# Attention and a maxout layer on one core: weights scaled by sixes, the first query blocks of four batches ahead, two sets of tokens in turn

## The chip, the core and the metric

The kernel runs on one core of a Trainium2 chip, in one launch. Its engines work side by side and are tied by semaphores: TensorE (PE, with its weight loads PEld), VectorE (DVE), ScalarE (ACT), GpSimd (POOL) and SyncE (SP). DMAs are issued here from SyncE's and from ScalarE's list. The metric is the device time of a run in microseconds.

## The reference

For 8 batches, 8 heads, 576 positions and 64 columns a head, in float32:

```python
scores = scale * np.matmul(q, k.transpose(0, 1, 3, 2))
cum = np.cumsum(np.maximum(s, 0.0), axis=-1)
bias = -(cum[:, :, :, None] - cum[:, :, None, :])
scores = np.where(causal, -1e9, scores + np.minimum(bias, 0.0))
attn = softmax(scores)                                  # over the keys
x = np.matmul(attn, v)  # heads side by side: 4608 tokens of 512 columns
h = np.maximum(np.maximum(x @ w1, x @ w2), x @ w3)      # 512 to 768
return h @ w_out                                        # 768 to 512
```

The four weight matrices arrive as 64-bit numbers, q, k, v and s as float32.

## The kernel before, in words

**Attention.** Two heads make a pair (`g`, four pairs a batch), and a *visit* is one batch, one pair and a list of query blocks of 128 (the fifth block is the last 64 positions). Batches that are in the array `qkv0` (its first dimension is `NB`, 2 before) are visited twice: first for the query blocks 0 and 1 alone (phase 0, 256 tokens), later for the blocks 2, 3 and 4 (phase 1, 320 tokens). The other batches are visited once for all five blocks. A *step* is one query block of one visit; there are 160.

A step runs over the engines in this order: the scores, in high and low parts (`scores`, TensorE, tiles `s`); their maximum (`highest`, VectorE, `nm`); the exponentials (`expo`, ScalarE); the reciprocal of their sum (`ri`, VectorE); the probabilities as a high half (`prh`, ScalarE) and a low half (`prl`, VectorE), both float16; their transposes by DMA from SyncE's list into `ph` and `pl` (tags `pTh`, `pTl`, one buffer for each phase); and, once a phase of a visit is complete, the products with v (`values`, TensorE, tile `av`), which ScalarE and VectorE bring into the token tile `x`, again as a high and a low half. Two score buffers are there, so the scores of step t+2 are written when those of step t are free.

**Experts.** When the four pairs of a batch's phase are done, its 256 or 320 tokens are a *set* (`add_set`), named by batch and phase: 2_1 is batch 2, phase 1. A set has 18 groups of 12 matmuls (`pm`, L593: six blocks `ft` of 128 hidden columns, three matrices each), of which ScalarE fetches the first (`m`, L607), VectorE maximises in the other two (L610), ScalarE and GpSimd split the result (`hh` L599, `hl` L600); and 4 output groups of 18 matmuls (`po`, L635), brought out by ScalarE (L643) and written by DMA. The groups wait in a list, `queue`, in the order of their sets. `run_group` takes the first, provided that its weights are there. How many go into a step is rationed: each step adds `STEP_NS` = 4800 ns less its own estimated time on TensorE to an account, and groups are issued while it is above zero. What is left after the last step runs at the end.

**Weights.** 24 blocks of 128 x 512 numbers in 64 bits, 18 for the hidden layer and 6 for the output. Each is loaded (`load_w`, tile `r`), put together as float32 from its two words (`decode1` on ScalarE L489, `decode2` on VectorE, three instructions, L494, L495, L498), and split into two float16 halves (`decode3` on ScalarE L552; `decode4`, on VectorE L566 or, for each third block, on GpSimd L563, L564). Ahead of the split stands a power of two by which they are scaled: from products of the blocks with themselves (`gram1`, TensorE, tile `gr`, L508), their maximum (`gram2`), and its spread over all partitions by a small matmul (`power`, tile `gm`). There is one scale for the 18 blocks and one for the 6, so no block of the 18 is split before all of them are loaded and decoded.

**Order.** Nothing is scheduled by a tool: each engine's list is written out by the loop over the steps and by two tables, `early` and `todo`, which name what else is done in a step (loads, preparations, weights). `begun`, `split` and `fetched` are the steps at which the weights' decode, split and load stand. SyncE's list holds the transposes, most loads of q, k and v and the writes of the outputs; the weights are loaded from ScalarE's list, but for the first few.

## Time and profile before

| | |
|---|---|
| median of 3 runs | 979.97 us (979.19 to 982.53) |
| the profiled run's own time | 981.28 us |
| its span, first to last instruction | 979.5 us |
| mean granted clock of TensorE in it | 0.948 |
| TensorE matmul, weight load busy | 867.9 us (89%), 657.7 us (67%) |
| VectorE, ScalarE, GpSimd busy | 566.5 us, 571.7 us, 182.3 us |
| DMA | 107.41 MB in all, 12.3 MB of them by ScalarE's queue |

The page gives each engine's busy time, and the same over 40 equal slices of the span in tenths. Matmuls are pipelined and overlap, so a time per matmul is better read from a stretch of them end to end than from the mean duration of one. A line such as L610 is a line of the kernel before; the number in brackets behind a busy time counts instructions.

### The profile page before, as it was taken

The page shows a single profiled execution, that of the slowest core. Times are in us where ns is not written, and L with a number is a line of the kernel's source. Part 1 is how long each engine was busy: PE and PEld are TensorE (multiplying, and loading weights), DVE is VectorE, ACT ScalarE, POOL GpSimd, SP SyncE. Part 2 cuts the span into 40 slices and gives each one's busy share as a digit, 9 for nine tenths or more (in the row PEclk, how much of TensorE's full clock was granted, in tenths as well). Part 3 has the DMA queues.
Part 4 walks back from the last instruction along what each step waited for, and adds up shares of the span by engine and source line. Part 5 has one row for each costly group of instructions (what it writes and reads, how often), then busy time and mean ns, then how long its engine had stood idle before and what let it go on. Part 6 is the DMA issues. An engine that isn't in the chain of part 4 may idle for free. (4 is left out here: it accounts for less than half of the span.)

```text
span 979.5 us, 20205 instructions
## 1 busy us (share of the span) xinstructions
PE 867.9 (89%) x7576; PEld 657.7 (67%) x7576; DVE 566.5 (58%) x1184; ACT 571.7 (58%) x1550; POOL 182.3 (19%) x231
## 2 busy tenths in 40 slices
PE   2446779897999959999999999999999999999998
PEld 1334557775666748767777767766776777777876
DVE  6797876656646565656565655555565655454111
ACT  4547666656566565666666666666566666665121
POOL 2003641212103010212121212112121212110111
PEclk9756879999999968999999999999999999999999
DMA  8962345476465565554745463645555474434000
GB/s 298 225 180 52 91 82 127 94 143 126 93 136 117 125 113 92 124 103 99 136 98 122 77 135 80 128 97 118 99 109 122 96 135 85 110 63 96 8 23 27
DMA packets 237810, 107.41 MB, mean 110 GB/s; under 512 B 216656, under 2 KB 225360, under 8 KB 237712
## 3 DMA queue, kind: packets, MB, share of 16 engines
q1 hardware_dynamic: 233680, 93.79, 46.1%
q10 hardware_dynamic: 4032, 12.32, 4.4%
q8 instruction: 60, 0.98, 0.5%
q14 instruction: 38, 0.31, 0.1%
...
## 5 line engine op out<-in xcount | busy, mean ns | idle before, releaser
L593 PE MATMUL pm<-x,w 128*128 128x256 f16 (+1 forms) x3456 | 458.8, 290 | 10.7 <-DVE x L468 5.8
L593 PEld LDWEIGHTS <-w 128*128 128x128 f16 x3456 | 333.8, 99 | 98.0 <-issue 10.6
L404 DVE SCALAR_TENSOR_TENSOR prl<-s,ri,prh 128x512 f16<-128x512 f32 (+3 forms) x288 | 152.8, 568 | 84.4 <-ACT prh L401 54.3
L401 ACT ACTIVATE prh<-s,ri 128x512 f16<-128x512 f32 (+3 forms) x288 | 141.9, 538 | 76.4 <-DVE ri L385 61.2
L600 POOL TENSOR_TENSOR hl<-m,hh 128x256 f16<-128x256 f32 (+1 forms) x96 | 71.4, 744 | 567.2 <-ACT hh L599 561.1
L352 DVE TENSOR_REDUCE nm<-s 128x1 f32<-128x576 f32 (+4 forms) x160 | 128.4, 803 | 63.1 <-PE s L325 57.9
L362 ACT ACTIVATE s<-s,nm 128x512 f32<-128x512 f32 (+4 forms) x288 | 150.6, 523 | 10.2 <-DVE nm L352 6.1
L610 DVE SCALAR_TENSOR_TENSOR m<-pm,m 128x256 f32<-128x256 f32 (+1 forms) x192 | 87.0, 453 | 117.4 <-PE pm L593 101.6
L635 PE MATMUL po<-hh,w 128*128 128x256 f16 (+1 forms) x768 | 151.4, 288 | 0.0
L635 PEld LDWEIGHTS <-w 128*128 128x128 f16 x1152 | 111.3, 99 | 27.4
L635 PE MATMUL po<-hl,w 128*128 128x320 f16 (+1 forms) x384 | 110.6, 288 | 0.0
L599 ACT ACTIVATE hh<-m 128x256 f16<-128x256 f32 (+1 forms) x96 | 42.3, 440 | 105.5 <-DVE m L610 105.3
L321 PE MATMUL s<-qkh 64*128 64x128 f32 (+3 forms) x256 | 56.3, 429 | 49.6 <-DVE prl L404 42.9
L263 POOL TENSOR_TENSOR qkl<-raw,qkh 128x576 fp32r<-128x576 f32 (+1 forms) x36 | 55.0, 1527 | 174.0 <-PE s L325 117.9
L321 PEld LDWEIGHTS s<-qkh 64*128 64x128 f32 x256 | 26.9, 196 | 80.4 <-ACT s L362 42.4
L607 ACT ACTIVATE m<-pm 128x256 f32<-128x256 f32 (+1 forms) x96 | 38.9, 405 | 64.8 <-PE pm L593 62.6
L468 DVE SCALAR_TENSOR_TENSOR x<-av,x 128x256 f16<-128x256 f32 (+1 forms) x64 | 29.0, 453 | 74.4 <-ACT x L467 74.3
L467 ACT ACTIVATE x<-av 128x256 f16<-128x256 f32 (+1 forms) x64 | 26.3, 410 | 75.4 <-PE av L457 75.3
L643 ACT ACTIVATE o<-po,os 128x256 f32<-128x256 f32 (+1 forms) x64 | 31.9, 498 | 51.5 <-PE po L635 48.1
L457 PE MATMUL av<-pl,vh 128*64 128x320 f16 (+3 forms) x384 | 57.1, 283 | 5.3 <-DMA pl<-prl 5.3
L457 PEld LDWEIGHTS <-vh 128*64 128x64 f16 x832 | 45.2, 113 | 23.7 <-issue 17.1
L457 PE MATMUL av<-ph,vh 128*64 128x320 f16 (+3 forms) x384 | 58.2, 291 | 0.1
(120 smaller groups left out, 1028.5 us busy)
## 6 DMA issues: line engine op xcount, KB each, us to landing
...
r<-in_w_dram ACTq DMA_DIRECT2D x20, 512.0 KB, 5.6
...
ph<-prh SPq DMA_TRANSPOSE x192, 3.2
pl<-prl SPq DMA_TRANSPOSE x192, 2.8
```

The source lines that it names most:

```text
L263: nc.gpsimd.tensor_tensor(out=r["lo"][:, cq:c1], in0=r["k"], in1=r["hi"][:, cq:c1].bitcast(F32), op=ALU.subtract)
L321: nc.tensor.matmul(ps[:, j, :nk], lhsT=lhsT, rhs=rt[rows], start=(n == 0), stop=False, skip_group_check=True)
L352: nc.vector.tensor_reduce(out=nm, in_=sc, axis=AX.X, op=ALU.max, negate=True)
L362: nc.scalar.activation(out=sc, in_=sc, func=AF.Exp, bias=nm[:, j:j + 1], accum_out=sm[:, j:j + 1])
L401: nc.scalar.activation(out=hi, in_=src, func=AF.Copy, scale=sc)
L404: nc.vector.scalar_tensor_tensor(out=lo, in0=src, scalar=sc, in1=hi, op0=ALU.mult, op1=ALU.subtract)
L457: nc.tensor.matmul(av[j * D:(j + 1) * D, c0:nq], lhsT=lt, rhs=rt, start=(n < 2), stop=(n >= len(todo) - 2), skip_group_check=True,)
L593: nc.tensor.matmul(pm[:, :nq], lhsT=w[:, wt, kt, :], rhs=xt, start=(n == 0), stop=(n == 3 * NKT - 1))
L599: nc.scalar.activation(out=st["hh"][:, ft, :nq], in_=m1[:, :nq], func=AF.Copy)
L600: nc.gpsimd.tensor_tensor(out=st["hl"][:, ft, :nq], in0=m1[:, :nq], in1=st["hh"][:, ft, :nq], op=ALU.subtract)
L610: nc.vector.scalar_tensor_tensor(out=m1[:, :nq], in0=pm[:, :nq], scalar=HSC, in1=m1[:, :nq], op0=ALU.mult, op1=ALU.max)
L635: nc.tensor.matmul(pm[:, :nq], lhsT=W[18 + ft][:, wt, dt, :], rhs=st[ht][:, ft, :nq], start=(n == 0), stop=(n == 3 * NFT - 1),)
```

## The change

The array `qkv0` holds four batches instead of two (`nb = 4`). Thereby 16 visits of the blocks 0 and 1 stand first, then 16 of the blocks 2, 3 and 4, then the other four batches as before.

The 24 weight blocks are scaled in four chunks of six in the order in which they are used, each chunk with its own power of two. So the first six can be split once they are loaded and decoded, and a hidden block's scale depends on its chunk; a factor (`rel`) on the output weights of that hidden block makes up for it, computed by GpSimd from the four scales. The decode, one block a step or less at first, is spread over the steps -2 to 26, the splits over 10 to 32; the low half is taken by VectorE for all blocks. The raw blocks share 12 buffers instead of having one each, and those from 2 on are loaded from SyncE's list, the last twelve as buffers come free.

`queue` is a list of sets, and `next_group` takes the next group of the first or, where that one's weights are not there, of the second set. The two sets have their own buffers `hh`, `hlo` and `m1`; outputs use the decode's buffers `t`. The token tiles use `x0` to `x5` and the raw buffers. In the visits for the blocks 0 and 1 alone, `ph` and `pl` alternate between two buffers from visit to visit. The spread of a scale (`spread_max`) is a step later than its maximum. In the first 32 steps the account gets 5600 ns a step, and the results of groups are fetched behind a step's `todo` instead of both ahead of it and behind it.

```diff
     def load_start(v, dma):
-        t = wpool.tile([P, 2 * N], F32, tag=f"w{18 + v}", name=f"st{v}")
-        dma(out=t[:, 0:768], in_=qkv0[0, visits[v][1]])
+        g = visits[v][1]
+        t = wpool.tile([P, N], F32, tag=f"r{RAW - NP + v}", name=f"st{v}")
+        dma(out=t, in_=qkv0[0, g, :, 0:512])
+        rv = io.tile([P, QKV - V0], F32, tag=f"rv{g}", name=f"rv{v}")[:, 0:256]
+        dma(out=rv, in_=qkv0[0, g, :, 512:768])
...
     def load_w(i, dma=None):
-        w = wpool.tile([P, 2 * N], F32, tag=f"w{i}", name=f"r{i}")
+        w = wpool.tile([P, 2 * N], F32, tag=f"r{i % RAW}", name=f"r{i}")
...
         if qb in (0, 2):
+            tag = v % 2 if visits[v][2][-1] == 1 else ph
             PT[v, ph] = [
-                att.tile([P, 4 + 4 * ph, PH[ph][1]], F16, tag=f"pT{c}{ph}", name=f"p{c}{t}", bufs=1) for c in "hl"
+                att.tile([P, 4 + 4 * ph, PH[ph][1]], F16, tag=f"pT{c}{tag}", name=f"p{c}{t}", bufs=1) for c in "hl"
             ]
...
-        if k < 2 * NB:
-            return moe.tile([P, 2, 2, nq], F16, tag=f"x{k}", name=name)
-        tag = f"w{10 + (k - 2 * NB) % 8}"
+        tag = f"x{k}" if k < 6 else f"r{(k - 6) % RAW}"
...
-    def gram1(kind, n, ids):
-        gr = ps_m.tile([P, 512], F32, tag="m", name=f"gr{kind}{n}")
-        for a, i in enumerate(ids):
+    def gram1(c):
+        gr = ps_m.tile([P, 512], F32, tag="m", name=f"gr{c}")
+        for i in range(6 * c, 6 * c + 6):
...
+    def scale_w(i):
+        return WS[chunk(i)] if i < 18 else WS["rel", (i - 18) // 2]
...
-        if by_pool(i):
-            ts = moe.tile([P, N], F32, tag="t", name=f"ts{i}", bufs=4)
-            nc.gpsimd.tensor_scalar(out=ts, in0=t, scalar1=sw, scalar2=None, op0=ALU.mult)
-            nc.gpsimd.tensor_tensor(out=w[:, 1], in0=ts, in1=w[:, 0], op=ALU.subtract)
-        else:
-            nc.vector.scalar_tensor_tensor(
-                out=w[:, 1], in0=t, scalar=sw, in1=w[:, 0], op0=ALU.mult, op1=ALU.subtract
-            )
+        nc.vector.scalar_tensor_tensor(
+            out=w[:, 1], in0=t, scalar=scale_w(i), in1=w[:, 0], op0=ALU.mult, op1=ALU.subtract
+        )
...
+        slot = 0 if ph else 1 if b >= NB else b % 2
+        wide = 256 if slot else 320
+        groups = []
...
-                queue.append((lambda ft=ft, i=i: h_group(ft, i), (3 * ft + i,), 12 * nq * NSEC))
+                groups.append((lambda ft=ft, i=i: h_group(ft, i), (3 * ft + i,), 12 * nq * NSEC))
...
+        queue.append(groups)
...
+    def next_group():
+        for groups in queue[:2]:
+            if all(i in W for i in groups[0][1]):
+                return groups
+        return None
+
     def ready():
-        return bool(queue) and all(i in W for i in queue[0][1])
+        return next_group() is not None
 
     def run_group():
-        f, _, c = queue.pop(0)
+        groups = next_group()
+        f, _, c = groups.pop(0)
         f()
         cost[0] -= c
+        if not groups:
+            queue.remove(groups)
...
-    begun = {i: (i - 1) // 2 - 1 for i in range(1, 18)}
-    begun.update({0: -2, 17: 6, 22: 7, 23: 8, 18: 9, 19: 10, 20: 11, 21: 12})
-    split = {i: 8 + i // 3 for i in range(18)}
-    split.update({i: 15 + (i - 18) // 3 for i in range(18, 24)})
+    begun = {0: -2, 1: -1, 2: 1, 3: 3, 4: 4, 5: 5}
+    begun.update({6: 7, 7: 9, 8: 11, 9: 12, 10: 13, 11: 14})
+    begun.update({12: 15, 13: 16, 14: 17, 15: 18, 16: 19, 17: 20})
+    begun.update({18: 22, 19: 22, 20: 23, 21: 23, 22: 24, 23: 25})
+    scaled = {0: 8, 1: 16, 2: 22, 3: 27}
+    split = {i: scaled[i // 6] + 2 + ((i % 6) if i < 6 else (i % 6) // 2) for i in range(NW)}
+    for c, t in scaled.items():
+        soon(t, gram1, c)
+        at(t, gram2, c)
+        soon(t + 1, spread_max, (c, "top"))
+        at(t + 1, wscale, c)
...
-    for i, t in fetched.items():
-        at(t, load_w, i, nc.scalar.dma_start)
+    for i in range(8, RAW):
+        at(max(2 * (i - 8) - 3, 0), load_w, i)
+    for i, t in split.items():
+        if i + RAW < NW:
+            at(t + 1, load_w, i + RAW)
...
-        cost[0] = min(cost[0] + STEP_NS - pe_cost(t), 4000.0)
+        cost[0] = min(cost[0] + (5600.0 if t < 2 * NP * NB else STEP_NS) - pe_cost(t), 4000.0)
...
-        drain()
-        flush()
+        if t >= 2 * NP * NB:
+            drain()
+            flush()
         for f, a in todo.get(t, ()):
             f(*a)
+        drain()
+        flush()
...
-    nb = 2
+    nb = 4
```

How the lists move, at three places. The first is VectorE's list from the maximum of step 5 on (`t` and `r` are a weight block being decoded, `am` a maximum over v, `vl` the low half of v). Before:

```order
L352 TENSOR_REDUCE nm5_465<-s5_464 128x2
L404 SCALAR_TENSOR_TENSOR prl4_508<-s4_377,ri4_505,prh4_507 128x128 x2
L494 TENSOR_SCALAR t9_499<-t9_499 128x512
L495 SCALAR_TENSOR_TENSOR t9_499<-r9_295,t9_499 128x512
L498 SCALAR_TENSOR_TENSOR r9_295<-r9_295,t9_499 128x512
L494 TENSOR_SCALAR t10_501<-t10_501 128x512
L495 SCALAR_TENSOR_TENSOR t10_501<-r10_297,t10_501 128x512
L498 SCALAR_TENSOR_TENSOR r10_297<-r10_297,t10_501 128x512
L290 SCALAR_TENSOR_TENSOR vl2_494<-st2_137,inv0_0_231,vh2_493 128x2x128
```

and of the change:

```order
L360 TENSOR_REDUCE nm5_418<-s5_417 128x2
L413 SCALAR_TENSOR_TENSOR prl4_449<-s4_362,ri4_446,prh4_448 128x128 x2
L500 TENSOR_SCALAR t3_440<-t3_440 128x512
L501 SCALAR_TENSOR_TENSOR t3_440<-r3_153,t3_440 128x512
L504 SCALAR_TENSOR_TENSOR r3_153<-r3_153,t3_440 128x512
L236 TENSOR_REDUCE am4_477<-rv4_254 128x1
L236 TENSOR_REDUCE am4_477<-rv5_383 128x1
L298 SCALAR_TENSOR_TENSOR vl2_435<-rv2_143,inv0_0_243,vh2_434 128x2x128
```

One weight block is decoded in the step where two were, and the blocks 9 and 10 come many steps later. The second place is VectorE's list around step 55 (`m` rows fetch an expert group, `x` a token tile). Before:

```order
L352 TENSOR_REDUCE nm54_4425<-s54_4424 128x1
L404 SCALAR_TENSOR_TENSOR prl53_4462<-s53_4387,ri53_4459,prh53_4461 128x4x128 x2
L468 SCALAR_TENSOR_TENSOR x18_0_4470<-av18_0_4446,x18_0_4470 128x256
L385 RECIPROCAL ri54_4491<-se54_4487 128x1
L352 TENSOR_REDUCE nm55_4474<-s55_4473 128x2
L404 SCALAR_TENSOR_TENSOR prl54_4494<-s54_4424,ri54_4491,prh54_4493 128x512
L404 SCALAR_TENSOR_TENSOR tl54_4495<-s54_4424,ri54_4491,tl54_4495 128x64
```

and of the change:

```order
L360 TENSOR_REDUCE nm54_4327<-s54_4326 128x2
L413 SCALAR_TENSOR_TENSOR prl53_4359<-s53_4250,ri53_4356,prh53_4358 128x3x128 x2
L625 SCALAR_TENSOR_TENSOR m13_0_4_4309<-pm3_0_4_2_4367,m13_0_4_4309 128x256
L298 SCALAR_TENSOR_TENSOR vl23_4346<-rv23_3385,inv1_1_3773,vh23_4345 128x640
L274 SCALAR_TENSOR_TENSOR qkl24_4402<-raw24_4092,qkh24_4350 128x384
L394 RECIPROCAL ri54_4462<-se54_4394 128x2
L360 TENSOR_REDUCE nm55_4381<-s55_4380 128x1
L413 SCALAR_TENSOR_TENSOR prl54_4465<-s54_4326,ri54_4462,prh54_4464 128x4x128 x2
L625 SCALAR_TENSOR_TENSOR m13_0_5_4473<-pm3_0_5_1_4420,m13_0_5_4473 128x256
```

Before, no expert group is in the list between the steps 53 and 58; in the change groups of set 3_0 are. In TensorE's list the change has, of expert groups, the 18 of 0_0 and the 18 of 1_0 before step 31, none in 31 to 33, and then some in every step: the eight output groups of those two sets, 2_0, 3_0, 0_1 and 1_1 but for two output groups by step 80. Before, the sets 0_0, 1_0, 0_1, 1_1, 2_0 and 2_1 stand by step 80. The third place is who issues the weights' loads. Before, ScalarE's list in step 5:

```order
L256 ACTIVATE qkh4_563<-raw4_422 128x256
L489 ACTIVATE t11_566<-r11_299 128x512
L489 ACTIVATE t12_568<-r12_345 128x512
L125 DMA r22_570<-in_w_dram 128x512
L125 DMA r23_572<-in_w_dram 128x512
L401 ACTIVATE prh5_589<-s5_464,ri5_587 128x2x128 x2
```

and of the change SyncE's, in the steps 20 to 22:

```order
L416 DMA_TRANSPOSE ph20_1544<-prh20_1548 128x2x128
L416 DMA_TRANSPOSE pl20_1545<-prl20_1549 128x2x128
L114 DMA rv14_1596<-in_qkv0_dram 128x256
L99 DMA raw13_1598<-in_qkv0_dram 128x512
L129 DMA r20_1608<-in_w_dram 128x512
L129 DMA r21_1610<-in_w_dram 128x512
L416 DMA_TRANSPOSE ph20_1544<-prh21_1668 128x4x128
L416 DMA_TRANSPOSE pl20_1545<-prl21_1669 128x4x128
```

The weights' loads stand between the transposes of one step and the next.

More of the change, by code (lines that the diff above doesn't have):

```diff
@@ L500, in decode2, with chunk, gram2, wscale @@
         )
[L502 to L504 removed]
+    def chunk(i):
+        return i // 6
+    def gram1(c):
+        gr = ps_m.tile([P, 512], F32, tag="m", name=f"gr{c}")
+        for i in range(6 * c, 6 * c + 6):
             top = raw_w[i].bitcast(BF16).rearrange("p (n t) -> p n t", t=4)[:, :, 1]
[L506 to L507 removed]
+            for k in range(NKT):
+                part = top[:, k * P:(k + 1) * P]
                 nc.tensor.matmul(
[L509 to L527 removed]
+                    gr[:, :P], lhsT=part, rhs=part,
+                    start=(i % 6 == 0 and k == 0), stop=(i % 6 == 5 and k == NKT - 1),
+                )
+        WS[c, "gram"] = gr
+    def gram2(c):
+        am = small.tile([P, 1], F32, tag="am1", name=f"amw{c}")
+        nc.vector.tensor_reduce(out=am, in_=WS.pop((c, "gram"))[:, :P], axis=AX.X, op=ALU.max)
+        WS[c, "top"] = power(am, f"w{c}")
+    def wscale(c):
+        mx = small.tile([P, 1], F32, tag="mx", name=f"mxw{c}")
+        nc.vector.tensor_reduce(out=mx, in_=WS.pop((c, "top"))[:, :P], axis=AX.X, op=ALU.max)
+        rt = const.tile([P, 1], F32, name=f"rt{c}")
         nc.vector.tensor_scalar(
@@ L531, in wscale2 @@
         )
-        sw = const.tile([P, 1], F32, name=f"sw{kind}")
+        sw = const.tile([P, 1], F32, name=f"sw{c}")
         nc.vector.reciprocal(out=sw, in_=rt)
         nc.vector.tensor_scalar(out=sw, in0=sw, scalar1=2.0 ** -56, scalar2=None, op0=ALU.mult)
-        WS[kind] = sw
+        WS[c] = sw
         nc.gpsimd.tensor_scalar(out=rt, in0=rt, scalar1=2.0 ** 56, scalar2=None, op0=ALU.mult)
-        WS[kind, "inv"] = rt
-        if kind == "d":
+        WS[c, "inv"] = rt
+        if c == 2:
+            low = const.tile([P, 1], F32, name="low")
+            nc.gpsimd.tensor_scalar(out=low, in0=WS[0], scalar1=WS[1], scalar2=None, op0=ALU.min)
+            nc.gpsimd.tensor_scalar(out=low, in0=low, scalar1=WS[2], scalar2=None, op0=ALU.min)
+            top = const.tile([P, 1], F32, name="top")
+            nc.gpsimd.tensor_scalar(out=top, in0=WS[0, "inv"], scalar1=WS[1, "inv"], scalar2=None, op0=ALU.max)
+            nc.gpsimd.tensor_scalar(out=top, in0=top, scalar1=WS[2, "inv"], scalar2=None, op0=ALU.max)
+            WS["top"] = top
+            for k in range(3):
+                f = const.tile([P, 1], F32, name=f"rel{k}")
+                nc.gpsimd.tensor_scalar(out=f, in0=WS[k, "inv"], scalar1=low, scalar2=None, op0=ALU.mult)
+                WS["rel", k] = f
+        if c == 3:
+            for k in range(3):
+                f = WS["rel", k]
+                nc.gpsimd.tensor_scalar(out=f, in0=f, scalar1=sw, scalar2=None, op0=ALU.mult)
             kw = const.tile([P, 1], F32, name="kw")
             nc.gpsimd.tensor_scalar(
-                out=kw, in0=rt, scalar1=WS["u", "inv"], scalar2=1.0 / HSC, op0=ALU.mult, op1=ALU.mult
+                out=kw, in0=rt, scalar1=WS["top"], scalar2=1.0 / HSC, op0=ALU.mult, op1=ALU.mult
             )
             WS["kw"] = kw
+    def scale_w(i):
+        return WS[chunk(i)] if i < 18 else WS["rel", (i - 18) // 2]
     def decode3(i):
@@ L582, in add_set @@
         u = f"{b}_{ph}"
-        xs = [(t[:, i, 0], t[:, i, 1]) for t in X.pop((b, ph)) for i in range(2)]
+        xs = [(t[:, i, 0, 0:nq], t[:, i, 1, 0:nq]) for t in X.pop((b, ph)) for i in range(2)]
         st = {}
+        slot = 0 if ph else 1 if b >= NB else b % 2
+        wide = 256 if slot else 320
+        groups = []
         def h_group(ft, i):
@@ L726 @@
         w = v - NP
[L727 to L731 removed]
+        at(first[w] + (4 if w % NP == 0 else 2), vmax, v)
     for v in range(NP, len(visits), NP):
@@ L738 @@
                 t = first[v] + 1 + (f is prep5) if v else -1
-            if f is prep5 and v >= NP and v + NP < len(visits):
+            if f is prep5 and v + NP < len(visits):
                 at(t, f, v)
@@ L742 @@
                 continue
-            if f is load and NP <= v < 2 * NP:
+            if f is load and v < NP * NB + 2:
                 t = first[v] - 6
             at(t, f, v, *([nc.scalar.dma_start] if f is load and v < NP + 2 else []))
-    at(8, wscale2, "u")
     for i, t in split.items():
```

80 lines of the change are left out of this document (23 added, 57 removed).

## The prediction

> **What bounds the kernel now.** I read the page's slices first, then busy times by stage.
>
> ```profile
> PE 867.9 (89%) x7576; PEld 657.7 (67%) x7576; DVE 566.5 (58%) x1184; ACT 571.7 (58%) x1550; POOL 182.3 (19%) x231
> PE   2446779897999959999999999999999999999998
> PEclk9756879999999968999999999999999999999999
> ```
>
> TensorE is at nine tenths or more from about 370 us to the end. It is poorly filled in the first seven slices of 24.5 us and again in slice 15 (343 to 367 us). I number a step by its maximum reduction nm (L352) and cut the span at such reductions:
>
> ```profile
> 13.20:127.20 114.00, 8.53 (x16) 0.75 0.56 144
> 127.20:479.80 352.60, 55.47 (x64) 0.94 0.56 115
> 479.80:899.10 419.30, 63.63 (x80) 1.00 0.52 104
> ```
>
> So steps 0 to 15 take 114.0 us (7.1 each), 16 to 79 take 352.6 (5.5), 80 to 159 take 419.3 (5.2), and 80.4 us follow. The engines in smaller stages (columns PE, PEld, DVE, ACT, POOL busy, clock, DMA share, GB/s):
>
> ```profile
> 13.20:34.90 21.70, 10.62 (x69) 8.52 (x70) 19.44 (x45) 14.99 (x43) 1.87 (x2) 1.00 0.99 256
> 34.90:72.80 37.90, 15.83 (x135) 12.81 (x135) 31.12 (x71) 18.22 (x54) 1.68 (x2) 0.59 0.74 195
> 72.80:127.20 54.40, 38.83 (x312) 29.92 (x311) 44.88 (x97) 35.44 (x94) 25.90 (x21) 0.76 0.27 64
> ...
> 164.70:265.40 100.70, 88.92 (x763) 66.50 (x761) 62.01 (x120) 63.20 (x158) 20.49 (x24) 0.97 0.61 124
> 343.10:369.80 26.70, 15.99 (x100) 12.18 (x102) 16.35 (x31) 17.64 (x48) 3.96 (x4) 0.60 0.63 118
> 503.60:609.50 105.90, 102.51 (x935) 77.84 (x933) 61.41 (x131) 66.00 (x184) 18.44 (x23) 1.00 0.53 109
> ```
>
> Three regimes. In the steady state (last row, one batch) TensorE is busy 102.5 of 105.9 us and sets the pace. In the first 114 us VectorE is busy 19.44 + 31.12 + 44.88 = 95.4 us, 84%, and TensorE 57% at clocks down to 0.59. From 343 to 370 us nobody is full. The counts of the expert matmuls (L593) say why:
>
> ```profile
> 13.20:127.20 114.00, 25.87 (x176) 19.25 (x177) 0.75 0.56 144
> 164.70:265.40 100.70, 53.45 (x386) 37.73 (x384) 0.97 0.61 124
> 343.10:369.80 26.70, 0.00 (x0) 0.00 (x0) 0.60 0.63 118
> ```
>
> From 343.1 to 369.8 us not one runs: the list is empty, because batch 2's sets are complete only at its last visit. So TensorE has too little it may do in two places, and its total work does not change with this edit. What the change can win is idle TensorE time.
>
> **Prices on TensorE.** The chain that ended last is nothing but expert work at full clock:
>
> ```profile
> 911.79 17.14 PE pm L593 x156
> 928.93 7.99 PE po L635 x72
> 936.91 29.34 PE pm L593 x216
> 966.25 9.79 PE po L635 x72
> ```
>
> A matmul takes 0.110 us at 256 columns (17.14 / 156, 7.99 / 72) and 0.136 at 320. A group of 12 costs 1.32 or 1.63 us, an output group of 18 2.0 or 2.45, a whole set 31.8 (18 x 1.32 + 4 x 2.0) or 39.1 (29.34 + 9.79). The batch of the steady row holds one of each, 70.9; the other 35.0 us are four visits, 8.75 each, stalls included. For the second half of a visit (query blocks 2 to 4) I use 164.7 to 265.4 us: 17 steps, 5.67 such halves, and besides the 386 matmuls (32 groups, 16 of each width, 47.2 us) four output groups (8.0). That leaves 45.5 us, 8.0 a half, or 5.9 if TensorE's idle 11.8 us are taken off. I take 6.0 for a filled TensorE, so 2.75 for the first half.
>
> **Stage one, steps 0 to 31.** The change visits blocks 0 and 1 of four batches, not two: 32 such steps, with the same 24 weights' decode spread over them. VectorE paid for the old stage, so I price the new one there:
>
> ```profile
> L385 DVE RECIPROCAL ri<-se 128x2 f32<-128x2 f32 x128 | 20.4, 160 | 37.9 <-ACT se L366 37.7
> L352 DVE TENSOR_REDUCE nm<-s 128x2 f32<-128x256 f32 x32 | 13.2, 412 | 10.4 <-PE s L325 10.4
> L352 DVE TENSOR_REDUCE nm<-s 128x2 f32<-128x512 f32 x32 | 21.8, 682 | 6.0 <-PE s L325 5.6
> L404 DVE SCALAR_TENSOR_TENSOR prl<-s,ri,prh 128x128 f16<-128x128 f32 x64 | 19.4, 345 | 12.8 <-ACT prh L401 9.3 <-DMA pl<-prl 2.8
> L404 DVE SCALAR_TENSOR_TENSOR prl<-s,ri,prh 128x256 f16<-128x256 f32 x64 | 27.8, 476 | 11.0 <-ACT prh L401 6.2 <-DMA pl<-prl 4.8
> L266 DVE SCALAR_TENSOR_TENSOR qkl<-raw,qkh 128x256 fp32r<-128x256 f32 x4 | 2.2, 548 | 0.0
> L290 DVE SCALAR_TENSOR_TENSOR vl<-rv,inv,vh 128x256 f16<-128x256 f32 x4 | 1.8, 474 | 0.0
> L228 DVE TENSOR_REDUCE am<-rv 128x1 f32<-128x256 f32 x4 | 1.5, 409 | 0.0
> L468 DVE SCALAR_TENSOR_TENSOR x<-av,x 128x256 f16<-128x256 f32 x32 | 13.3, 414 | 0.4 <-ACT x L467 0.3
> L566 DVE SCALAR_TENSOR_TENSOR w<-r,swu,w 128x512 f16<-128x512 f32 x12 | 10.8, 936 | 0.0
> L240 DVE TENSOR_REDUCE mx<-gmv 128x1 f32<-128x128 f32 x10 | 2.8, 281 | 0.4 <-PE gmv L219 0.4
> L610 DVE SCALAR_TENSOR_TENSOR m<-pm,m 128x256 f32<-128x256 f32 x96 | 40.4, 421 | 56.4 <-PE pm L593 44.2 <-ACT s L362 5.1 <-ACT m L607 4.0
> ```
>
> A half visit costs VectorE 2 x 0.16 + 0.41 + 0.68 + 2 x 0.345 + 2 x 0.476 + 0.55 + 0.47 + 0.41 + 0.41 = 4.9 us. Eight more are 39. The lower halves of the weights all move to VectorE: 20 stand before step 32, where 12 of VectorE's stood in the old stage; 8 x 0.94 = 7.5 (an upper price: this row shares its time with GpSimd's part of the same job, which goes). Groups before step 32: 36, against 176 / 12 = 14.7; two of three end on VectorE, 14 more x 0.42 = 6. Two more weight scales and two more value scales, each two reductions of 128 columns (0.28) and some four instructions of one column (0.16, as ri), 1.0 to 1.2 us; less three Gram reductions that go (seven were, four are), about 3. Decode, 24 weights, unchanged. VectorE: 95.4 + 39 + 7.5 + 6 + 3 = 151 us, 4.7 a step. At the old stage's 84% that is 180 us, 5.6 a step.
>
> Why not less efficient than before: a wait goes. In the old stage SyncE's list of transposes stood still (start, duration):
>
> ```profile
> 25.41 1.23 SPq L407 DMA_TRANSPOSE pl<-prl  x1
> 38.27 1.17 SPq L407 DMA_TRANSPOSE ph<-prh  x1
> ...
> PE s L321 <- DVE prl L404: 37.5, 12, 6.7
> ```
>
> Between visit 0's last transposes and visit 1's lie 12.9 us, since one buffer pT held both and av0 had to finish; behind it probs' buffers, prl, and the scores waited (37.5 us up to 130 us, in the waits). Now two visits alternate. Weights also load as buffers come free, where the first 60 us had the DMA engines 99% and 74% busy. Why not more efficient: ScalarE was busy 14.99 + 18.22 + 35.44 = 68.7 us, 4.3 a step, stays near that, and each step goes to and fro between the two. TensorE has 16 x 2.75 + 36 x 1.32 + some 5 for the Gram products = 96 us at full clock; at the 0.59 of the row above 164, still below 180. So two edits cost nothing here while that slack stands: groups are rationed by 5600 ns a step, and their results are fetched behind the decode instead of ahead of it, so that a fourth group in a step waits for one of three PSUM buffers. Without the slack each such step would lose about one group, 1.3 us.
>
> [...]
>
> Bounds for stage one: 166 (90%, the share in 13.2 to 34.9 us), and 228 (the old 7.1 us a step). I take 180, nearest to what VectorE showed over the whole old stage. The prologue (13.2) keeps its work.
>
> **Stage two, steps 32 to 79.** Sixteen second halves, 16 x 6.0 = 96. By the instruction list the expert work here is the 8 output groups of the first two sets (16.0), two whole sets of 256 (63.6) and two of 320 less two output groups (78.2 - 4.9): 153. Sum 249, plus 5 for steps 31 to 33, which have no groups while the last weights are split: 254 us, 5.3 a step. From 33 to 158 no step is without a group, so the hole at 343 us goes. Bounds: 16 x 5.9 + 153 = 247; and the pace of 164.7 to 265.4 us (100.7 / 17 = 5.92), 284.
>
> **Stage three, from step 80 on.** The same attention as before, 979.5 - 479.8 = 499.7 us. Expert work left: before sets 3_0 and 3_1 and four batches; now 2_1, 3_1, two output groups of 1_1, and four batches: 39.1 - 31.8 + 4.9 = 12.2 us more. 512. Double buffers of hh, hlo and of m1 could win at most TensorE's idle 3.4 us a batch, 14; I count none, since the idle time ahead of the scores' weight loads (500 to 800 us) ends with other things:
>
> ```profile
> PEld s L321 <- issue: 7.3, 28, 0.7
> ...
> PEld s L341 <- ACT s L362: 6.4, 6, 1.6
> ...
> L628 POOL TENSOR_SCALAR os<-p,kw 128x1 f32<-128x1 f32 x16 | 5.2, 325 | 0.0
> ```
>
> The turn of two sets changes order, not work. GpSimd's ten new one-column factors stand off the path beside an engine busy 19%; uncovered, 10 x 0.33 = 3.3 us.
>
> **Sum.** 13.2 + 180 + 254 + 512 = 959 us of span, against 979.5. The profiled run took 981.28, the median is 979.97, so I carry the difference: 979.97 - 20.3 = **959.7 us**.
>
> **Rivals.**
>
> *Weights hold up the transposes (slower).* Weights 12 to 23 are now issued by SyncE, in one list with the transposes.
>
> ```profile
> r<-in_w_dram ACTq DMA_DIRECT2D x20, 512.0 KB, 5.6
> r<-in_w_dram SPq DMA_DIRECT2D x4, 512.0 KB, 9.2
> ```
>
> If each pushes its next transpose back by 9.2 - 5.6 = 3.6 us and nothing hides it, 12 x 3.6 = 43 us: 1003. It decides from 1.7 us a load. For it: no weight stood between transposes before. Against: the 9.2 is from the time when the DMA engines were 99% busy, and a transpose has a step's slack before av. [...] 6%.
>
> *Stage one keeps 7.1 us a step (slower).* The price is in the dialogue of the engines, not VectorE's sum: 228 instead of 180, 1008. It decides from 200. Against: steps 0 to 3 took 21.7 us with two decodes each, 5.4 a step, more VectorE work than the new average. 7%.
>
> *Stage two stays at 5.92 (slower by less than 1%).* 284, 990. For it: that row is the same mix of work, TensorE 88% busy. Against: its first part ran below full clock, its sets came one at a time. 8%.
>
> *The clock holds stage one.* The third slice of the page shows a granted clock of five tenths. Kept there through all of stage one, TensorE's 96 us become 192, more than VectorE's 180: 972. It decides below 96 / 180 = 0.53. For it: twelve steps without a group at the start. Against: the old stage as a whole had 0.75. [...] 8%.
>
> *More gain.* 166, 247 and half of the 14: 13.2 + 166 + 247 + 505 = 931. For it: the weights' rows were priced with GpSimd's share in them. 14%.
>
> *It does not do what it says:* the list shows the groups moved, so only a hole elsewhere; within 0.3% of before, 3%.
>
> **How the numbers follow.** 54% for the forecast, its own range 943 to 975, 8% for the clock, within it. The range 932 to 984 takes in half of the greater gain and leaves the slow cases out. A measurement of this kernel tells a change from none at about 0.3% (3 us). Faster: forecast, clock, gain and some of the mild ends of the rivals, 0.81; same 0.05; slower 0.14.
>
> **What would show it.** Right: nm 32 at about 193 us, nm 80 at about 447; VectorE 80% or more busy in stage one; no stretch of 20 us without L593's successor after 200 us; about 92 us after nm 159 instead of 80. Wrong: nm 32 after 215 us (transposes late by SyncE's list, or TensorE full below 0.6 of its clock), or stage two over 270 us with TensorE under 90% busy.

## The result, and the profile after

The changed kernel takes 994.62 us (median of 4 runs, 993.62 to 995.7); the kernel before, beside it, 981.25 (4 runs, 979.19 to 984.71). The ratio is 1.0134 (95% interval 1.0110 to 1.0158): 1.3% **slower**, where 959.7 was forecast. The profiled execution has a span of 993.9 us.

Busy times and slices of the changed kernel, from its page (TensorE, and the granted clock in tenths):

```profile
PE 879.7 (89%) x7580; PEld 664.1 (67%) x7580; DVE 574.7 (58%) x1231; ACT 580.5 (58%) x1574; POOL 171.1 (17%) x235
PE   3567787799888987998899999999999999998998
...
PEclk9977896889999999999999999999999999998999
```

Half of what was expected is to be seen at once. The first slices are fuller (3567787799 where 2446779897 stood), and the five of slice 15 is gone. But of the slices 11 to 20 six are eights and one a seven, where all but that five were nines, and TensorE, for four more matmuls, is busy for 879.7 instead of 867.9 us.

The same stages as in the prediction, cut at the maxima (now L360) of the steps 0, 32, 80 and 159 (columns PE, PEld, DVE, ACT, POOL busy, clock, DMA share, GB/s):

```profile
13.50:191.80 178.30, 124.24 (x1042) 96.71 (x1042) 138.33 (x348) 115.80 (x354) 29.49 (x43) 0.85 0.52 129
191.80:479.60 287.80, 254.88 (x2168) 191.48 (x2165) 173.97 (x331) 178.72 (x442) 53.06 (x62) 0.94 0.57 121
479.60:894.90 415.30, 403.91 (x3628) 301.84 (x3627) 239.57 (x505) 260.98 (x724) 71.26 (x83) 1.00 0.54 108
894.90:993.90 99.00, 92.97 (x736) 71.47 (x733) 16.34 (x35) 21.20 (x48) 11.18 (x17) 0.97 0.12 28
```

13.5 + 178.3 + 287.8 + 514.3 (415.3 + 99.0) = 993.9, against 13.2 + 180 + 254 + 512 in the forecast. **The whole error is stage two**, 287.8 for 254. Step 80 begins at 479.6 us; before it began at 479.8. By then the change has done less expert work, 12.2 us of it by the prediction's prices, and that work comes after step 80. So one of the prediction's own signs of being wrong is there, stage two over 270 us with TensorE under 90% busy (254.88 of 287.80 is 89%), and one of being right is missed by little: VectorE is 78% busy in stage one, not 80% or more.

Stage two has 287.80 - 254.88 = 32.9 us in which TensorE does nothing. Its waits there, from the waits of 191.8 to 479.6 us (us in total, times, longest):

```profile
PE s L349 <- DVE prl L413: 29.1, 14, 3.0
...
PE s L349 <- DVE am L242: 2.0, 2, 1.5
...
PE s L329 <- DVE prl L413: 1.7, 1, 1.7
```

L349 writes the scores of block 4, the third and last step of a visit to the blocks 2, 3 and 4. It waits up to 3 us for the low half of the probabilities of block 2, which frees its score buffer. There are 16 such visits in stage two, and 31.1 of its 32.9 idle us (29.1 and 2.0; the second line is the same place, released by another instruction) stand there. In stage three, whose 16 visits have five steps, the same wait for `prl` takes 4.5 us in all. The timeline of one of the 16 (start, duration, engine, line, what it writes from what; in brackets the idle time of its engine before it and what ended that):

```profile
392.96 1.79 PE L608 MATMUL pm<-x,w 128*128 128x320 f16 x12
393.12 0.20 ACT L374 ACTIVATE se<-sm 128x2 f32<-128x2 f32 x1
...
393.35 0.17 DVE L394 RECIPROCAL ri<-se 128x2 f32<-128x2 f32 x1 [0.67 <-ACT se L374]
...
393.54 0.82 ACT L293 ACTIVATE vh<-rv,inv 128x640 f16<-128x640 f32 x1
394.26 0.51 ACT L263 ACTIVATE qkh<-raw 128x384 fp32r<-128x384 f32 x1
...
394.67 0.67 ACT L264 ACTIVATE qkh<-raw 128x576 fp32r<-128x576 f32 x1
395.25 1.04 ACT L410 ACTIVATE prh<-s,ri 128x384 f16<-128x384 f32 x2
...
396.32 1.14 DVE L413 SCALAR_TENSOR_TENSOR prl<-s,ri,prh 128x384 f16<-128x384 f32 x2 [1.68 <-ACT prh L410]
...
397.61 0.36 PE L349 MATMUL s<-qkh 128*128 128x256 f32 x1 [2.85 <-DVE prl L413]
```

Two things meet. `ri` is ready at 393.52, but `prh` starts at 395.25, because two preparations stand ahead of it on ScalarE: `vh` (`prep4`, 0.82 us) and `qkh` (`prep2`, 0.51 and 0.67). They stand 1 and 4 steps ahead of the visit that they serve. Where a visit has five steps these are different steps of a visit; where it has three, 1 and 4 are the same place in it: both stand at the end of the step of block 4, and so right ahead of `prh` of the next visit's block 2. (The first visit of each batch is the exception: its `prep4` comes two steps later. Of the 16 waits, the four in these visits are 2.85, 0.67, 0.49 and 1.52 us, the first of them where stage two begins and no group may run yet; the other twelve are 1.10 to 3.05, 2.13 on average.) And TensorE's list holds one group there (12 matmuls), which is over at 394.75, and then block 4's scores, so it stands still for 2.85 us with work in `queue`.

The kernel before has the same wait in its 8 such visits (steps 16 to 39). Its waits from 164.7 to 265.4 us, the stretch on which the forecast's 6.0 us rests:

```profile
PE s L341 <- DVE prl L404: 10.2, 5, 2.4
...
PE s L321 <- DVE tl L404: 1.1, 2, 0.9
...
PE s L341 <- DVE am L234: 0.5, 1, 0.5
```

10.2 + 1.1 + 0.5 are the 11.8 us that were "taken off" there. The change doubled the number of such visits.

### The profile page after: what moved, and what is told of

It reads as the page before. It is cut to its first block, busy times and chain, and to the rows that moved or that the text cites. A ratio compares the mean times of both kernels' runs of the same rounds, so it can differ in the third digit from the quotient of the medians.

```text
span 993.9 us, 20309 instructions
## 1 busy us (share of the span) xinstructions
PE 879.7 (89%) x7580; PEld 664.1 (67%) x7580; DVE 574.7 (58%) x1231; ACT 580.5 (58%) x1574; POOL 171.1 (17%) x235
## 5 line engine op out<-in xcount | busy, mean ns | idle before, releaser
L608 PE MATMUL pm<-x,w 128*128 128x256 f16 (+1 forms) x3456 | 466.8, 292 | 9.5 <-DVE w L578 8.9
L413 DVE SCALAR_TENSOR_TENSOR prl<-s,ri,prh 128x384 f16<-128x384 f32 (+3 forms) x288 | 153.0, 568 | 97.3 <-ACT prh L410 62.5
L410 ACT ACTIVATE prh<-s,ri 128x384 f16<-128x384 f32 (+3 forms) x288 | 142.0, 538 | 80.6 <-DVE ri L394 67.9
L360 DVE TENSOR_REDUCE nm<-s 128x2 f32<-128x1024 f32 (+4 forms) x160 | 128.2, 801 | 49.1 <-PE s L333 44.9
L370 ACT ACTIVATE s<-s,nm 128x384 f32<-128x384 f32 (+4 forms) x288 | 150.6, 523 | 9.1 <-DVE nm L360 4.9
L650 PEld LDWEIGHTS <-w 128*128 128x128 f16 x1152 | 112.2, 99 | 31.1 <-issue 1.6
L271 POOL TENSOR_TENSOR qkl<-raw,qkh 128x576 fp32r<-128x576 f32 (+1 forms) x44 | 59.8, 1358 | 172.7 <-ACT qkh L264 98.9
L474 DVE SCALAR_TENSOR_TENSOR x<-av,x 128x256 f16<-128x256 f32 (+1 forms) x64 | 29.1, 454 | 67.5 <-ACT x L473 67.5
L463 PEld LDWEIGHTS <-vh 128*64 128x64 f16 x832 | 45.2, 114 | 20.6 <-issue 15.0
```

Source lines behind the costliest of these rows:

```text
L271: nc.gpsimd.tensor_tensor(out=r["lo"][:, cq:c1], in0=r["k"], in1=r["hi"][:, cq:c1].bitcast(F32), op=ALU.subtract)
L360: nc.vector.tensor_reduce(out=nm, in_=sc, axis=AX.X, op=ALU.max, negate=True)
L370: nc.scalar.activation(out=sc, in_=sc, func=AF.Exp, bias=nm[:, j:j + 1], accum_out=sm[:, j:j + 1])
L410: nc.scalar.activation(out=hi, in_=src, func=AF.Copy, scale=sc)
L413: nc.vector.scalar_tensor_tensor(out=lo, in0=src, scalar=sc, in1=hi, op0=ALU.mult, op1=ALU.subtract)
L463: nc.tensor.matmul(av[j * D:(j + 1) * D, c0:nq], lhsT=lt, rhs=rt, start=(n < 2), stop=(n >= len(todo) - 2), skip_group_check=True,)
```

## The experiments

The questions were whether this wait is the lost time, which of its two halves sets it, and whether stage one was right for the reason given. "Stage two" is the time from the maximum of step 32 to that of step 80, "the wait" TensorE's idle time ahead of block 4's scores in it. Both are those of the one execution that was profiled, which for some kernels lies 2 to 6 us off the median; where a kernel was run several times, its times spread over 2 to 9 us. So of the kernels that were run once only changes of 10 us and more say something by themselves. The changed kernel itself was not run again beside these.

**Preparation `prep2` one step earlier.** `qkh` moves out of the step that it shares with `vh`.

```diff
             t = first[v] - e
+            if f is prep2 and visits[v][2][0] == 2 and v >= NP * NB + 2:
+                t -= 1
```

> The changed kernel, with prep2 (ScalarE: high parts of q and k, 1.2 us) of the visits for blocks 2, 3 and 4 one step earlier, five steps ahead instead of four; nothing else. Theory A, collision: in a three-step visit the offsets 1 (prep4, ScalarE 0.8 us) and 4 (prep2) fall into the same step, so prh and prl of block 2, and by them the scores of block 4, come 2 us late while TensorE has nothing else in its list. Then TensorE's wait at the scores of block 4 falls from 29 us (14 times) to under 12, stage two (steps 32 to 79) from 288 to about 270, the time from 994.6 to about 976. Theory B, pace by ration: a step gets 4800 ns of TensorE work, less than the 6.0 us that a step of the attention chain takes; the wait moves to another block and the time stays at 990 or above.

982.28 us (10 runs, one of which took 2916.48 us; the median of the other nine is 982.14), ratio to the kernel before 1.0022 (0.9997 to 1.0046), without that one. Windows and waits of stage two:

```profile
192.10:464.00 271.90, 247.12 (x2166) 187.31 (x2163) 173.76 (x330) 178.22 (x442) 52.81 (x62) 0.97 0.59 128
```

```profile
PE s L349 <- DVE prl L413: 20.4, 13, 2.9
```

15.9 us of stage two go in the profiled execution, which was the fastest of the ten; the median falls by 12.3 us, and the change is no longer slower than the kernel before by more than the measurement tells. The wait falls by a third, to 20.4 us, where under 12 was expected: `vh` is still ahead of `prh`, and the list still holds one group there. Half of the stage's gain is not idle time at all: TensorE's busy time falls from 254.9 to 247.1 us, at a granted clock of 0.97 instead of 0.94 (the last section).

**Preparation `prep4` one step earlier instead.** The other one of the pair.

```diff
             t = first[v] - e
+            if f is prep4 and visits[v][2][0] == 2:
+                t -= 1
```

> The changed kernel with prep4 (the high part of v, ScalarE 0.8 us) two steps ahead instead of one in the three-step visits; prep2 stays. It parts the same two works at the other end. Theory A: stage two falls by about as much as 0.8 of 2.0 us of the collision takes, 16 visits x 0.8 = 10 to 13 us: about 982. Theory B: no change.

984.56 us (one run; 979.71 before beside it). Stage two 276.2, the wait on `prl` 29.1 to 22.4 us. Either one of the two may be moved, which is what a collision predicts and a fault of one of them alone would not.

**One of the two made longer.** `vh` is computed twice in the three-step visits, the second time over the first.

```diff
-        nc.scalar.activation(out=vh, in_=r["rv"], func=AF.Copy, scale=inv)
+        for _ in range(2 if visits[v][2][0] == 2 else 1):
+            nc.scalar.activation(out=vh, in_=r["rv"], func=AF.Copy, scale=inv)
```

> The changed kernel with ScalarE's vh computed twice (the same values into the same tile) in the 15 or 16 three-step visits; 0.82 us of added work on an engine that is 62% busy in stage two. Theory A, ScalarE's list in that step is on the chain to the scores of block 4: stage two grows by about 16 x 0.82 = 13 us, to 301. Theory B, the pace comes from the ration: ScalarE has room, stage two stays within 3 us of 288.

1010.7 us (one run; 980.26 before beside it). Windows and waits of stage two (L350 is here what L349 is above):

```profile
193.70:495.90 302.20, 257.25 (x2162) 192.90 (x2163) 173.86 (x330) 191.64 (x458) 52.97 (x62) 0.93 0.54 115
```

```profile
PE s L350 <- DVE prl L414: 39.9, 14, 4.4
```

Stage two is 14.4 us longer. In the twelve visits where `vh` stands ahead of `prh` of block 2, the wait grows by 0.68 to 1.32 us each, 0.90 on average, where `vh` takes 0.82; in the first visits of the four batches, where it stands elsewhere, it does not grow (2.85, 0.71, 0.49 and 0.51 us). ScalarE is busy 63% of stage two in this run, and yet at this one place what is added to it comes out as a wait of TensorE. So its list there is on the path.

**A second group ahead of block 4's scores.** ScalarE's list stays; TensorE gets something to do.

```diff
-        if ready() and cost[0] > 0:
-            run_group()
+        for _ in range(2 if visits[v][2][0] == 2 and qb == 2 else 1):
+            if ready() and cost[0] > 0:
+                run_group()
```

> The changed kernel with up to two expert groups instead of one ahead of the scores of block 4 in the three-step visits; the ration stays, so the same groups stand in stage two, some of them earlier in TensorE's list. If the idle 31 us there are only a matter of where groups stand, TensorE's wait at that place falls by one group each, 1.3 to 1.6 us x 16 = about 20 us, and the time to about 975. If the chain of prl sets the visit's length whatever TensorE does, the wait moves to the scores of blocks 2 and 3 or the ends of the steps, and the time stays above 990.

976.4 us (one run; 980.26 beside it). Stage two:

```profile
194.50:460.90 266.40, 245.29 (x2162) 188.07 (x2163) 174.18 (x331) 178.39 (x442) 54.61 (x62) 0.97 0.62 130
```

```profile
PE s L349 <- DVE prl L413: 13.7, 9, 2.9
```

Here 21.4 us go, without an instruction less on ScalarE. By this one run, and by the next kernel, the stall has two necessary halves, a late `prl` and an empty place in TensorE's list.

**Both.**

```diff
+            if f is prep2 and visits[v][2][0] == 2 and v >= NP * NB + 2:
+                t -= 1
...
+        for _ in range(2 if visits[v][2][0] == 2 and qb == 2 else 1):
+            if ready() and cost[0] > 0:
+                run_group()
```

> The changed kernel with prep2 a step earlier in the three-step visits and up to two groups ahead of the scores of block 4 there; ration as in the change. Alone they took stage two from 288 to 272 and to 266. If both relieve one and the same wait (prl of block 2 late, nothing in TensorE's list), together they leave the idle time there at a few us and stage two at about 258, the time at about 966. If they are two causes, the gains of 16 and 21 add up: stage two 250, which is what TensorE's work alone takes.

**970.42 us** (6 runs, 968.38 to 973.29), 980.78 before beside it (17 runs): ratio 0.9892 (0.9868 to 0.9915), 1.1% faster than the kernel before, and 24 us under the 994.62 of the changed kernel. Windows and waits of stage two, and the same place of the same visit (the list now has 24 matmuls there):

```profile
195.30:456.30 261.00, 243.81 (x2162) 187.32 (x2163) 173.98 (x331) 178.19 (x442) 54.11 (x62) 0.97 0.64 133
```

```profile
PE s L349 <- DVE prl L413: 7.4, 7, 2.9
```

```profile
378.60 3.42 PE L608 MATMUL pm<-x,w 128*128 128x320 f16 x24
...
382.21 0.36 PE L349 MATMUL s<-qkh 128*128 128x256 f32 x1 [0.19 <-DVE prl L413]
```

Stage two takes 261.0, 26.8 less than in the changed kernel and 7 more than the forecast's 254. The two edits do not add (15.9 + 21.4 = 37.3), since each takes from the same wait.

**More groups allowed in stage two.** The account gets 5600 ns a step until step 79 instead of step 31: does the ration keep the list empty?

```diff
-(5600.0 if t < 2 * NP * NB else STEP_NS)
+(5600.0 if t < 5 * NP * NB else STEP_NS)
```

> The changed kernel with 5600 ns a step instead of 4800 in the steps 32 to 79 too (until step 79 all steps have 5600), so more expert groups stand in stage two's lists and fewer at the end. Theory B, ration: TensorE's idle 33 us of stage two are filled, the stage stays at about 288 and the end comes some 25 us earlier, about 970. Theory A, collision: the wait is at one place of the list, ahead of the scores of block 4, where no group stands; further groups come elsewhere and lengthen the stage by what they take (38 us more of work, perhaps half of it in the idle time), the tail shortens by the same 38: 980 to 992.

984.72 us (9 runs), 1.0049 (1.0028 to 1.0069). Stage two:

```profile
196.00:487.00 291.00, 275.02 (x2390) 207.67 (x2391) 180.22 (x341) 182.47 (x454) 57.81 (x67) 0.98 0.57 121
```

TensorE's idle time in it falls from 32.9 to 16.0 us, with 222 more matmuls done in it. The time is what the collision forecast (980 to 992), but not quite for its reason: more groups do come to stand ahead of block 4's scores, and the wait there falls from 31.1 to 13.2 us. And steps 80 to 159, where it was idle for 11.4 of 415.3 us, now have it idle for 21.9 of 418.6: the groups spent early are missing there. Of the 16.9 us 10.5 are given back.

**`prep2` earlier and the larger ration.**

```diff
+            if f is prep2 and visits[v][2][0] == 2 and v >= NP * NB + 2:
+                t -= 1
...
-(5600.0 if t < 2 * NP * NB else STEP_NS)
+(5600.0 if t < 5 * NP * NB else STEP_NS)
```

> The changed kernel with both edits: prep2 a step earlier in the three-step visits, and 5600 ns a step until step 79. If both causes stand side by side, it is faster than each alone, 955 to 965. If the collision is all, the time is that of the first edit, about 976. If the ration is all, that of the second.

975.43 us (10 runs), 0.9957 (0.9941 to 0.9972). That is 7 us below the first edit alone, and far from the 955 to 965 of two causes side by side. Stage two has 9.0 us of idle TensorE, the steps 80 to 159 have 21.5:

```profile
193.20:476.30 283.10, 274.12 (x2390) 207.53 (x2391) 180.56 (x341) 183.38 (x454) 58.20 (x67) 0.98 0.59 124
476.30:892.60 416.30, 394.84 (x3520) 295.80 (x3520) 236.32 (x497) 258.04 (x718) 67.45 (x81) 0.98 0.53 107
```

**All three edits.**

```diff
+            if f is prep2 and visits[v][2][0] == 2 and v >= NP * NB + 2:
+                t -= 1
...
+        for _ in range(2 if visits[v][2][0] == 2 and qb == 2 else 1):
+            if ready() and cost[0] > 0:
+                run_group()
...
-(5600.0 if t < 2 * NP * NB else STEP_NS)
+(5600.0 if t < 5 * NP * NB else STEP_NS)
```

> The same with 5600 ns a step until step 79. If the ration was a cause beside the place of the groups, some 5 to 10 us below the run without it. If it only filled the same idle time, the same time or slightly more, since stage three's idle time rose from 11 to 21 us with it.

973.7 us (6 runs), 0.9924 (0.9903 to 0.9946), beside the 970.42 of the two edits without the ration. The wait is down to 2.8 us, but the steps 80 to 159 are idle for 22.2. With the place in the list filled, the ration only moves idle time; where the place was empty, it filled a part of it and was worth 10 us alone and 7 us beside `prep2`.

**`prep3` one step earlier as well** (`qkl`, on GpSimd and VectorE), with `prep2` and the ration.

```diff
+            if f in (prep2, prep3) and visits[v][2][0] == 2 and v >= NP * NB + 2:
+                t -= 1
```

> The changed kernel with both edits (prep2 a step earlier in three-step visits, 5600 ns until step 79) and prep3 too a step earlier there, so that VectorE's low part of q (0.55 us) does not fall into the step of prep5 (0.88 us). If VectorE's work there is on the chain as ScalarE's was, some 5 us below 975.4; TensorE's idle time in stage two is down to 9 us, so no more. If not, 975.

982.45 us (10 runs), 1.0024 (1.0008 to 1.0039): worse than without it. The wait is 10.1 us instead of 6.2. In its profile `qkl` on VectorE now stands ahead of `prl` of block 2, where it stood behind it, and may delay it; no run tells it apart.

**The kernel before with `prep2` earlier** in its three-step visits (for six of the 8; in the changed kernel it was 14 of 16).

```diff
             t = first[v] - e
+            if f is prep2 and visits[v][2][0] == 2 and v >= NP * NB + 2:
+                t -= 1
```

> The kernel before, with prep2 of its three-step visits (8 of them, two batches) one step earlier. Theory A: half as many such visits as the changed kernel has, so about half of its gain, 6 to 12 us off 980, and TensorE's wait at the scores of block 4 before 265 us, 12.6 us in 6 waits, falls to under 6. Theory B: no change beyond 0.3%.

979.88 us (10 runs), 0.9997 (0.9977 to 1.0017): no change. In its profile the steps 16 to 39 take 143.1 instead of 146.4 us and the wait falls from 13.1 to 9.6, where 6 to 12 us of the time and a wait under 6 were expected: a miss. For each visit that is 0.4 us, against 1.0 in the changed kernel, and the median shows nothing of it. Why is open.

**Three batches in the array** (12 + 12 visits ahead of the rest).

```diff
-    nb = 4
+    nb = 3
```

> The changed kernel with three batches instead of four ahead (24 steps of blocks 0 and 1, then 12 three-step visits). Theory A, the three-step visits cost 1.9 us of waiting each: four of them fewer, but the weights' splits then overlap with them (steps 24 to 32) and one set less is ready for them. I expect 985 to 995; if the number of three-step visits is not the price, no change or slower than 995.

977.37 us (one run; 979.71 beside it), below the 985 to 995 that were expected: a miss to the good side. Its 24 first steps take 126.5 us (5.3 each), its 36 steps of second halves 224.9 (6.2 each). So a step of a three-step visit is at least as dear there as in the change (287.8 / 48 = 6.0), and there are fewer of them: step 80 begins at 473.3 us, where it began at 479.8 before and at 479.6 in the change.

**Three batches, `prep2` earlier, and 5600 ns to step 79.**

```diff
-    nb = 4
+    nb = 3
...
+            if f is prep2 and visits[v][2][0] == 2 and v >= NP * NB + 2:
+                t -= 1
...
-(5600.0 if t < 2 * NP * NB else STEP_NS)
+(5600.0 if t < 80 else STEP_NS)
```

> The changed kernel with three batches ahead instead of four, prep2 a step earlier in the three-step visits, and 5600 ns a step until step 79. With three batches alone one look gave 977.4 (stage one 126.5 for 24 steps, TensorE idle 38.5 us in the 36 steps after). If collision and ration are what hold that stretch, its idle time falls to about 20 and the time to about 960, below the 975.4 that the two edits gave with four batches. If the stretch is held by the weights that are split in it, it stays at about 975.

978.25 us (8 runs), 0.9976 (0.9964 to 0.9988). The wait in the second halves falls from 25.3 to 13.4 us, and the time does not fall with it: a miss. The traces show a part of why: TensorE's idle time falls from 38.5 to 26.6 us in these 36 steps and rises from 12.4 to 20.6 in the steps 60 to 159, as it did with four batches. Of the wait that is left, 10.1 us are two waits of 6.2 and 3.8 near its start.

**One pair of buffers for the transposes.** In the changed kernel, the visits of stage one share one buffer again.

```diff
-            tag = v % 2 if visits[v][2][-1] == 1 else ph
+            tag = ph
```

> The changed kernel with one buffer pT for blocks 0 and 1 as before, instead of two in turn. By the prediction's step, the alternation is what lets stage one run at 5.6 us a step: without it each visit's first transposes wait for the products of the visit before. Stage one then takes 200 us or more instead of 178, and the time is 10 to 25 us longer than 994.6. If the buffer was not what held the old stage, stage one stays at 178.

994.77 us (one run), stage one:

```profile
13.80:193.40 179.60, 125.64 (x1037) 96.79 (x1039) 138.27 (x349) 116.24 (x354) 29.41 (x43) 0.90 0.49 124
```

179.6 for 178.3: the second buffer is worth next to nothing.

**Two buffers in the kernel before.**

```diff
-tag=f"pT{c}{ph}"
+tag=f"pT{c}{v % 2 if visits[v][2][-1] == 1 else ph}"
```

> The kernel before with two buffers pT in turn for the visits of blocks 0 and 1, nothing else. In the changed kernel one buffer instead of two cost nothing (stage one 179.5 against 178.4). If the single buffer held the kernel before, where av0 stood behind Gram products that waited for the decode, its first 16 steps shorten from 114 by 5 us or more. If not, VectorE's work held them, and they stay within 2 us.

981.26 us (10 runs), 1.0008 (0.9990 to 1.0027). Its old stage one, and the transposes that stood at 38.27 us:

```profile
13.40:128.80 115.40, 65.06 (x526) 51.44 (x528) 95.86 (x210) 68.34 (x191) 29.69 (x25) 0.76 0.62 143
```

```profile
25.66 1.29 SPq L407 DMA_TRANSPOSE pl<-prl  x1
30.86 1.18 SPq L407 DMA_TRANSPOSE ph<-prh  x1
```

The pause of 12.9 us shrinks to 5, and the stage still takes 115.4 us (114.0 before). VectorE's busy time is the same, 95.9. So the pause was there, and was not what set the time of the old stage.

**Weights from ScalarE's list.** The loads of the blocks 12 to 23 leave SyncE's list of transposes.

```diff
-            at(t + 1, load_w, i + RAW)
+            at(t + 1, load_w, i + RAW, nc.scalar.dma_start)
```

> The changed kernel with the loads of the weights 12 to 23 issued from ScalarE's list instead of SyncE's. If these loads hold up the transposes, stage one shortens by 5 us or more (12 loads, up to 3.6 us each). If they are hidden, as the forecast held, it stays within 2 us of 178.3, and issuing costs ScalarE 12 x 0.4 us; ScalarE then waits in its list for the raw buffer to come free, which could cost the same 5 us the other way.

991.52 us (one run; 979.71 before beside it), stage one:

```profile
13.60:193.40 179.80, 127.14 (x1042) 98.06 (x1042) 138.40 (x349) 115.94 (x354) 29.46 (x43) 0.83 0.53 128
```

Stage one is unmoved (179.8 for 178.3), so the loads among the transposes cost it nothing that shows. Stage two is 5 us shorter (282.7) in this one run, which is left open.

## Why the prediction was wrong

**The step that failed** is the price of a second half of a visit, in "Stage two": "That leaves 45.5 us, 8.0 a half, or 5.9 if TensorE's idle 11.8 us are taken off. I take 6.0 for a filled TensorE". The idle time was taken off without asking what ended it. 10.7 of the 11.8 us were the wait of L341, which belongs to the three-step visit itself, so sixteen such visits bring sixteen of them. The forecast reasoned as though TensorE were idle there for want of groups. There were groups; they were not at that place in its list. With the row's own 8.0 the sum would have been 16 x 8.0 + 153 + 5 = 286 us, where 287.8 were measured.

The sizes: 249 us of work and 5 for the start were set against 254.9 busy and 32.9 idle. With the wait mostly gone the same matmuls take 243.8 busy and 17.2 idle, 261.0 in all. So the forecast's sum was the price of a stage two in which nothing waits, and the two edits of the best kernel come within 7 us of it. The first rival of that stage, "Stage two stays at 5.92" with 284 us and 990, is what happened (287.8, 994.6). Its argument, the same mix of work, was right; the argument held against it, that its first part ran below full clock, was no reason: the row's clock of 0.97 is two stretches of 3.4 us at half clock, which begin at 174.5 and 246.2 us, 0.9 and 1.5 us after waits of L341 of 2.4 and 2.3 us had ended. So that half clock, too, stood behind waits (the last section). It had 8%.

**Stage one** came out at 178.3 for 180 by luck, through two errors that cancel: VectorE had 138.3 us of work instead of 151, and filled 78% of the stage instead of 84%. The lower halves were priced at 0.94 us, an upper price indeed: in the kernel before, `decode4` took VectorE 0.74 us at 97.95 us and 1.65 at 98.61, beside GpSimd's L564; in the change it takes 0.74 in the median. The reason given for its efficiency, the pause of the transposes behind one buffer, is refuted twice: without the second buffer the new stage takes 179.6, with it the old one 115.4. That VectorE's share carries over from the old stage to the new, roughly, is all that the runs support. (The stage's lower bound, 166, should have read 151 / 0.90 = 168; nothing hangs on it.)

**Stage three** came out at 514.3 for 512. The 12.2 us of expert work that move behind step 80 are the difference to 499.7, but for 2.4.

**The rivals.** The weights' loads on SyncE's list cost stage one nothing that shows: they land in 4.5 us, where four of them took 9.2 before, and moving twelve of them away leaves the stage as it is.

```profile
r<-in_w_dram SPq DMA_DIRECT2D x22, 512.0 KB, 4.5
```

The clock did not hold stage one: 0.85, well over the rival's 0.53. "It does not do what it says" is half true: the hole at 343 us went, as the list showed, and the idle time of TensorE up to step 80 did not fall with it. The windows of the kernel before, for all engines:

```profile
13.20:127.20 114.00, 65.28 (x514) 51.24 (x515) 95.44 (x209) 68.65 (x191) 29.45 (x25) 0.75 0.56 144
127.20:479.80 352.60, 317.85 (x2736) 236.57 (x2735) 210.06 (x424) 221.75 (x584) 65.96 (x76) 0.94 0.56 115
```

It was 114.0 - 65.3 = 48.7 us in the steps 0 to 15 and 352.6 - 317.9 = 34.7 in 16 to 79, together 83.4; now it is 54.1 + 32.9 = 87.0. So the expected gain turned into a new wait: the long hole went, and the idle time came back in pieces of 0.5 to 3 us.

## What to carry to other kernels

Idle time may be taken off a measured price only when the wait that ended it has been named and the change removes that wait; otherwise it belongs to the work and is multiplied with it. Jobs that stand a fixed number of steps ahead of the next visit meet in one step when those numbers are equal modulo the visit's length, so a change in the mix of visits calls for a look at each engine's list in one visit of each kind. And a full queue did not fill TensorE, which works its list in order (it stood still for 2.85 us up to 397.61 us with groups in `queue`): the work must stand at the place of the wait.

## What the runs showed of the chip

A wait of 2 to 3 us mostly cost TensorE more than its length. After the wait of 2.85 us shown above, the next group of 12 matmuls took 3.10 us where the last had taken 1.79:

```profile
399.12 3.10 PE L608 MATMUL pm<-x,w 128*128 128x320 f16 x12
```

From 210 us on, stage two has eight waits of over 2 us at L349, of 2.06 to 3.05. With seven of them comes a stretch of 3.41 us at a granted clock of 0.50, which begins between 0.29 us before the wait's end and 1.40 behind it. These stretches begin at 234.55, 251.61, 289.16, 323.29, 360.84, 398.39 and 470.07 us; in this profile they are whole multiples of 3.413 us apart, to 0.01 us. In the 3.41 us just ahead of each of the seven TensorE was busy for 0.78 to 1.40 us. The eighth wait, of 2.82 us up to 379.43, has no such stretch: in the 3.41 us up to 377.91, six times 3.413 ahead of 398.39, TensorE was busy for 2.11 us, in the 3.41 behind for 1.89, and the clock stayed at 1.00. Why this wait cost no clock was not shown; no run tests it. The rows around the wait shown above, and around the eighth:

```profile
394.98:398.39 3.41, 0.78 (x6) 0.81 (x7) 2.07 (x4) 2.96 (x8) 1.98 (x2) 1.00 0.28 47
398.39:401.80 3.41, 3.41 (x16) 2.06 (x15) 0.73 (x2) 0.00 (x0) 0.00 (x0) 0.50 0.50 150
...
374.50:377.91 3.41, 2.11 (x18) 1.21 (x14) 1.32 (x3) 3.38 (x9) 0.63 (x2) 1.00 0.74 98
377.91:381.32 3.41, 1.89 (x15) 1.63 (x16) 3.18 (x7) 2.12 (x7) 1.37 (x2) 1.00 0.26 41
381.32:384.74 3.42, 3.42 (x32) 2.40 (x32) 2.16 (x4) 1.44 (x3) 0.00 (x0) 1.00 0.41 137
```

In the kernel before, of the four waits of over 2 us at L341 from 164.7 to 265.4 us, of 2.28 to 2.38, two are followed by such a stretch (at 174.5 and 246.2 us); after the other two, of 2.28 us up to 226.82 and of 2.32 up to 264.00, the clock is 1.00.

Seven times 3.41 us at a clock of 0.50 come to an estimated 12 us. The best kernel, which has no such stretch after the stage's first 14 us (its clock is 1.00 from 209.3 to 456.3 us), is busy 254.9 - 243.8 = 11.1 us less for nearly the same matmuls (2162 and 2168 records); so of its 26.8 us in stage two 15.7 are waits and 11.1, by this estimate, clock. The forecast priced the clock in stage one, where TensorE is thin, and not here, where it is nine tenths busy. The shortest wait that came with a slow stretch is that of 2.06 us up to 469.13; in the 3.41 us ahead of that stretch TensorE was busy for 1.35.
